# Moving the norm of the last 896 tokens one stage sooner and spreading its steps

## The chip, the cores and the metric

One core of a Trainium2 chip runs the kernel. The metric is device time in microseconds for one execution. The engines are TensorE (PE; its weight loads are shown as PEld), VectorE (DVE), ScalarE (ACT), GpSimd (POOL) and SyncE (SP), which issues DMAs. All have queues of their own and run their instructions in order; semaphores tie them together.

## What is computed

Attention over short local and strided masks, then a feed-forward layer, then a gated feed-forward layer with an RMS norm, for 2304 tokens of 512 features. The change lies in the last layer:

```python
def _moe2_ref(x, w_gate, w_val, w_out, rms_g):
    rms = np.sqrt(np.mean(x * x, axis=-1, keepdims=True) + 1e-06)
    xn = x / rms * rms_g
    g = xn @ w_gate
    silu = g * (1.0 / (1.0 + np.exp(-g)))
    val = xn @ w_val
    return (silu * val @ w_out).astype(np.float32)
```

Here d_model is 512 and d_ff is 1536. Every product is made of three products of fp32r halves (high x high, high x low, low x high).

## The kernel before, in words

The last layer runs over the tokens in three passes: 512 tokens (the loop with `pe_gv`), then two passes of 896 tokens, `j = 0` (the second pass) and `j = 1`. A pass of 896 tokens has six stages, `p = 0` to `5`, each for two blocks of 128 columns of `w_gate` and `w_val`. In a stage the two products x @ w are made as seven smaller ones on sums of quarter matrices (Strassen's scheme in Winograd's form): `Stage.run` goes through the product groups m = 1, 2, 5, 6, 3, 7, 4, and each group is 6 matmuls for `w_gate` and 6 for `w_val`, of 448 columns. Groups 1, 6, 7 and 4 collect in one pair of PSUM banks (P), groups 5 and 3 in another (R), group 2 in a pair Q. Between the groups DVE and ACT read the banks:

- `keep` (L1050, ACT) copies the bank of group 1, 5 and 6 to SBUF;
- `add` (L1040, L1043, DVE) adds a copy to the bank of groups 2, 3 and 7, in the order gate, val; then L1026 (ACT) makes the silu, `mul` (L1031, DVE) the product, L1035 (ACT) its high half and L1036 (DVE) its low half;
- after group 4, L1026 and L1031 read the bank itself.

A bank is written again only after its readers: group 4 after L1040 and L1043 of group 7, group 1 of the next stage after L1026 and L1031 of group 4. In each stage `outs` also makes seven output products of the stage before it (6 matmuls of 512 columns each: two after group 5, two after group 7, three after group 4); L1099 (ACT, p = 0 of the output) or L1101 (DVE) adds them to `osum`. These, the pair Q and the norm's product `ps_r` share four banks.

After each group stands a `tick`. It issues DMAs of weights (`fetch`, `put`), in the second pass it moves the decoding of the weights on (`decode.to`: per stage four times L276 on ACT, L277 and L278 on DVE, and twice a batch on POOL of four L290, two L264 and two L265), and takes one step of the generator `pg`. That generator is `prep_s`, the norm of the 896 tokens of the next pass. It works in place on one SBUF tile x2 and goes through two halves (512 and 384 tokens):

- step 1 loads x (L919, four DMAs on SP);
- per half, steps of squares (L925, L927 on ACT, L928 on DVE), high and low half of their sum (L931, L932), an empty step, the product with ones on PE (`ps_r`), then on DVE the mean (L941), the start value (L945, L948) and three Newton steps of the inverse root (L952, L953, L954 each), last the scaling of x (L957, four times, two a step).

That is 23 steps and an end. In the last stage, p = 5, the first tick runs what is left of `pg`, and then each tick calls `conv(m)`: casts and sums of the quarters of x for the next pass (L971 on POOL, L990 on ACT, L991 on DVE).

PE and SP take their instructions in the order in which the program issues them. The order on DVE, ACT and POOL is set by a scheduler when the kernel is built, from its own estimates; so where a step is issued moves instructions of other steps on these engines as well.

Of the kernel before, what the change touches and what calls it, by code (L numbers as in the profile page):

```python
# [33 lines left out]
def attn_moe_moe_kernel(  # L34
# [42 lines left out]
    NJ = (NT - R0) // (2 * HT)  # L77
    NP = FB // 2

    def runs(s):  # L80

        r = []
        for i, (b, t) in enumerate(subs[s]):
            if r and r[-1][0] == b and r[-1][1] + r[-1][2] == t:
                r[-1][2] += 64
            else:
                r.append([b, t, 64, 64 * i])
        return r
# [34 lines left out]
    for s in range(len(subs)):  # L123
        if len(runs(s)) > 1 or s in LANES:
            _, t0, n, _ = runs(s)[0]
# [199 lines left out]
    class Store:  # L325


        n = 0
# [533 lines left out]
    def preps():  # L862
        yield from prep_s(0, [(0, R0)], bank_m, pbr)
        x = xt["raw"]
        t = mid.tile([128, 2, 4, 512], F32R, tag="xs", name="xn")
        for c in range(4):
            nc.scalar.copy(out=t[:, 0, c], in_=x[:, c, :R0])
            nc.vector.tensor_tensor(out=t[:, 1, c], in0=x[:, c, :R0], in1=t[:, 0, c].bitcast(F32), op=ALU.subtract)
            yield
        xn[0] = t  # L870
        yield from prep_s(R0, HALVES, bank_m, pbx)
        for m in (1, 2, 5, 6, 3, 7, 4):
            conv(m)
            yield
# [88 lines left out]
    def conv(m):  # L963

        x = xt["raw"]
        b = {(k, h): x[:, 2 * k:2 * k + 2, HT * h:HT * (h + 1)] for k in range(2) for h in range(2)}

        def comb(name, p, q, out=None):
            if out is None:
                out = tmp[0].tile([128, 2, 512], F32, tag="w", name="tr")[:, :, :HT]  # L970
            nc.gpsimd.tensor_tensor(out=out, in0=p, in1=q, op=ALU.subtract)  # L971
            xt[name] = out
            return out

        if m == 1:
            v = b[0, 0]
        elif m == 2:
            v = b[1, 0]
        elif m == 3:
            v = b[1, 1]  # L980
        elif m == 5:
            v = comb("t1", b[0, 1], b[0, 0])
        elif m == 6:
            v = comb("t2", b[1, 1], xt.pop("t1"))
        elif m == 7:
            v = comb("t3", b[1, 1], b[0, 1])
        else:
            v = comb("t4", b[1, 0], xt["t2"], xt["t2"])
        t = xt[m]
        nc.scalar.copy(out=t[:, 0], in_=v)  # L990
        nc.vector.tensor_tensor(out=t[:, 1], in0=v, in1=t[:, 0].bitcast(F32), op=ALU.subtract)  # L991
# [16 lines left out]
    class Stage:  # L1008
# [37 lines left out]
        def keep(self, x):  # L1046
# [5 lines left out]
            return r  # L1052

        def run(self, outs, tick):
            P, Q, R = {}, {}, {}
            self.both(1, P, True)
            if (self.j, self.p) == (0, 0):
                second()
            m1 = self.keep(P)
            tick(1)  # L1060

            def q():
                self.both(2, Q, True)
                self.add((0, 0), Q, m1)
                tick(2)
# [64 lines left out]
    xq, first_units, pg = [], units[:3], None  # L1130
# [87 lines left out]
    for g, f, a, e in units:  # L1218
# [38 lines left out]
        if g == NG - 1:  # L1257
            if f == 2:
                pg = preps()
# [41 lines left out]
    pg = iter(())  # L1301
    for j in range(NJ):
        for p in range(NP):
            first, last, end = (j, p) == (0, 0), p == NP - 1, (j, p) == (NJ - 1, NP - 1)
            me, nxt = pairs[p], pairs[(p + 1) % NP]
            st = Stage(j, p)

            def tick(m):
                n = (1, 2, 5, 6, 3, 7, 4).index(m)
                if first and n == 3:  # L1310
                    for t in range(R0 // 128):
                        nc.sync.dma_start(out=out[t * 128:t * 128 + 128, :], in_=osum[:, t])
                if n in (1, 5):
                    me.fetch((6,) if n == 1 else (7, 8))
                if j == 0:
                    decode.to(10 + 10 * (7 * p + n + 3) // 7)
                    if n in (3, 5):
                        for kd in range(2):
                            me.put((2 if n == 3 else 4) + kd)
                if not end and n == 4:  # L1320
                    nxt.fetch((0, 1))
                if not end and (j > 0 or last) and n in (5, 6):
                    nxt.fetch((2, 3) if n == 5 else (4, 5))
                next(pg, None)
                if last and j + 1 < NJ:
                    for _ in pg:
                        pass
                    conv(m)

            if p == 2 and j + 1 < NJ:  # L1330
                pg = prep_s(R0 + 2 * HT * (j + 1), HALVES, bank_x, pbx)

            def outs(n):
                for _ in range(min(n, len(todo))):
                    o, t = todo.pop(0)
                    o.out(t)

            st.run(outs, tick)
            todo += [(st, t) for t in ((4, 5, 6, 3, 0, 1, 2) if end else range(7))]
# [99 lines left out]
```

## Time and profile before

| | us |
|---|---|
| median of 3 runs (lowest to highest) | 889.43 (888.55 to 890.35) |
| the profiled execution | 887.7 |
| its span | 885.9 |
| PE busy | 868.8 |
| DVE busy | 668.5 |
| ACT busy | 397.9 |
| POOL busy | 280.0 |

The second pass of the last layer begins at some 556 us; its stages p = 1 to p = 5 start at 576.7, 603.3, 630.3, 659.2 and 686.2 us. In the rows below a time in the first place is us from the span's start and the second is the duration; "x4" is four instructions in one row; an entry in brackets is the idle time before and what ended it. L numbers are lines of the kernel before; in the changed kernel lines from L1325 on are one higher, and none that is named here is affected.

### The profile page before, as it was taken

To read this page: it belongs to the slowest core of one execution; us is meant where nothing else is said; L and a number is where in the kernel's file an instruction comes from. 1 tells how busy PE (TensorE), PEld (TensorE's weight loads), DVE (VectorE), ACT (ScalarE), POOL (GpSimd) and SP (SyncE) were. 2 spreads that over 40 slices of the span, in tenths; PEclk is the share of its full clock that TensorE was granted. 3 is DMA by queue.
4 is the path that set the end of the run, shared out by engine and by line. 5 is a ranking of instruction groups with operands and counts; after the bars stand their busy time and mean duration, and the time that the engine had idled before them with its cause. 6 is when DMAs were issued, how large, how long until landed. Compare 5 with 4: busy or idle time off the path is not lost.

```text
span 885.9 us, 14105 instructions
## 1 busy us (share of the span) xinstructions
PE 868.8 (98%) x5091; PEld 739.7 (83%) x5091; DVE 668.5 (75%) x1376; ACT 397.9 (45%) x897; POOL 280.0 (32%) x315
## 2 busy tenths in 40 slices
PE   6999999999999999999999999999999999999998
PEld 4888888888998887888887888888878988888986
DVE  5999788888779887179978898576997953445444
ACT  6987643332544333265637553355332533422320
POOL 0000147695276952000000569676442400000000
PEclk8999999999999999999999999999999999999999
DMA  9955224311313000199828777799659139955002
GB/s 328 379 196 173 77 73 151 111 50 36 116 54 110 28 16 1 46 291 346 280 72 270 279 250 270 252 415 364 232 179 349 48 114 355 397 168 166 1 0 84
DMA packets 58566, 157.84 MB, mean 178 GB/s; under 512 B 9536, under 2 KB 20672, under 8 KB 58496
## 3 DMA queue, kind: packets, MB, share of 16 engines
q1 hardware_dynamic: 57344, 155.89, 50.0%
q10 hardware_dynamic: 1152, 1.05, 0.3%
q8 instruction: 40, 0.66, 0.3%
q14 instruction: 30, 0.25, 0.1%
HBM read 119.16 MB, written 37.75 MB: 177 GB/s over the span
## 4 chain that ended last, share of the span: by engine, by line
PE 82%; DVE 8%; POOL 5%; ACT 2%; issue 1%; DMA 1%; SPq 0%; DVEq 0%; POOLq 0%; ACTq 0%
PE ps_x L147 21%; PE ps_h L147 21%; PE ps_pr L147 18%; PE ps_o L147 12%; POOL pr L629 4%; PE ps_m L147 4%; PE ps_q L147 3%; DVE so L669 3%; DMA raw<-in_w_in_dram 1%; PE ps_s L147 1%; POOL pr L662 1%; PE ps_v L147 1%; ACT sm L416 1%; PE ps_p L437 1%; DVE x L957 0%
## 5 line engine op out<-in xcount | busy, mean ns | idle before, releaser
L147 PE MATMUL ps_h<-xs,w 128*128 128x512 f32 (+1 forms) x984 | 213.4, 365 | 0.7 <-DVE tg L814 0.7
L147 PE MATMUL ps_x<-g,w 128*128 128x512 f32 (+1 forms) x984 | 214.0, 366 | 0.0
L147 PEld LDWEIGHTS ps_h<-xs,w 128*128 128x128 f32 x984 | 169.0, 189 | 30.6 <-DVE tg L814 1.1
L147 PEld LDWEIGHTS ps_x<-g,w 128*128 128x128 f32 x984 | 168.6, 189 | 30.0 <-issue 0.2
L147 PE MATMUL ps_pr<-xt,wt 128*128 128x448 f32 x576 | 123.1, 366 | 2.2 <-DVE s L1040 1.4
L629 POOL TENSOR_TENSOR pr<-sk,sq 128x256 f32<-128x256 f32 (+2 forms) x101 | 82.5, 852 | 131.8 <-DMA sq<-in_q_str_dram 126.4
L147 PE MATMUL ps_o<-wt,p 128*128 128x512 f32 x504 | 120.2, 390 | 0.0
L147 PEld LDWEIGHTS ps_pr<-xt,wt 128*128 128x128 f32 x576 | 107.9, 188 | 13.5 <-DVE s L1040 2.2
L147 PEld LDWEIGHTS ps_o<-wt,p 128*128 128x128 f32 x504 | 94.6, 188 | 18.7
L820 ACT CAST g<-tg 128x512 fp32r<-128x512 f32 (+1 forms) x82 | 46.6, 568 | 108.9 <-DVE tg L814 108.8
L662 POOL TENSOR_TENSOR pr<-sv,se 128x288 f32<-128x288 f32 (+12 forms) x104 | 69.7, 691 | 56.7 <-DVE so L669 19.8
L1050 ACT COPY u<-ps_pr 128x448 f32<-128x448 f32 x72 | 38.2, 533 | 84.8 <-PE ps_pr L147 84.7
L814 DVE SCALAR_TENSOR_TENSOR tg<-ps_h,tg 128x512 f32<-128x512 f32 (+1 forms) x82 | 50.8, 619 | 28.0 <-ACT tg L809 28.0
L669 DVE TENSOR_REDUCE so<-pr 128x16 f32<-128x272 f32 (+11 forms) x104 | 65.0, 653 | 8.7 <-POOL pr L662 8.4
L971 POOL TENSOR_TENSOR tr<-x 128x896 f32<-128x896 f32 x4 | 15.1, 3765 | 171.1 <-DMA raw<-in_w_gate_dram 153.9
L809 ACT ACTIVATE tg<-ps_h 128x512 f32<-128x512 f32 (+1 forms) x82 | 44.2, 539 | 48.1 <-PE ps_h L147 48.1
L1101 DVE SCALAR_TENSOR_TENSOR osum<-ps_o,osum 128x512 f32<-128x512 f32 x70 | 47.9, 687 | 21.6 <-PE ps_o L147 20.9
L825 DVE TENSOR_TENSOR g<-tg,g 128x512 fp32r<-128x512 f32 (+1 forms) x82 | 55.3, 677 | 10.8 <-ACT g L820 10.2
L147 PE MATMUL ps_pr<-xt,wo 128*128 128x448 f32 x288 | 60.8, 366 | 0.2 <-ACT u L1050 0.2
L147 PEld LDWEIGHTS ps_pr<-xt,wo 128*128 128x128 f32 x288 | 54.0, 188 | 5.2 <-ACT u L1050 0.6
L184 ACT CAST w<-ct 128x512 fp32r<-128x512 f32 x68 | 42.1, 619 | 30.3 <-DVE ct L177 28.2
L634 DVE TENSOR_REDUCE sc<-pr 128x4 f32<-128x256 f32 (+2 forms) x101 | 43.8, 437 | 12.1 <-POOL pr L629 11.6
(110 smaller groups left out, 1201.4 us busy)
## 6 DMA issues: line engine op xcount, KB each, us to landing
wt<-w SPq DMA_DIRECT2D x84, 512.0 KB, 5.9
raw<-in_w_out_dram SPq DMA_DIRECT2D x28, 512.0 KB, 6.1
raw<-in_w_gate_dram SPq DMA_DIRECT2D x24, 512.0 KB, 5.9
raw<-in_w_val_dram SPq DMA_DIRECT2D x24, 512.0 KB, 6.8
w<-w SPq DMA_DIRECT2D x24, 512.0 KB, 6.6
w<-wo SPq DMA_DIRECT2D x24, 512.0 KB, 8.2
raw<-in_w_in_dram SPq DMA_DIRECT2D x16, 512.0 KB, 9.9
out_dram<-osum SPq DMA_DIRECT2D x18, 256.0 KB, 2.1
```

The source lines that it names most:

```text
L147: nc.tensor.matmul(out_, lhsT, rhs, start=start, stop=stop, skip_group_check=True)
L184: nc.scalar.copy(out=self.t[:, 0].rearrange("p c f -> p (c f)"), in_=self.b)
L629: nc.gpsimd.tensor_tensor(out=pr, in0=self.k[:, a:e, :], in1=self.q[:, c - c0:c - c0 + 1, :].to_broadcast([128, e - a, D]), op=ALU.mult,)
L634: pend.append(lambda: nc.vector.tensor_reduce(out=s[:, c - c0, a:e], in_=pr, axis=AX.X, op=ALU.add))
L662: nc.gpsimd.tensor_tensor(out=pr, in0=self.v[:, 0:c + 1, a:e], in1=self.e[:, c - c0, 0:c + 1].unsqueeze(2).to_broadcast([128, c + 1, e - a ...
L669: pend.append(lambda: nc.vector.tensor_reduce(out=o[:, c - g0, a:e], in_=pr.rearrange("l c d -> l d c"), axis=AX.X, op=ALU.add))
L809: nc.scalar.activation(out=t, in_=h_of[g, f, a], func=ACTF.Tanh, scale=WS)
L814: nc.vector.scalar_tensor_tensor(out=t, in0=h_of.pop((g, f, a)), scalar=WS, in1=t, op0=ALU.mult, op1=ALU.subtract)
L820: nc.scalar.copy(out=t[:, 0], in_=t_of[g, f, a])
L825: nc.vector.tensor_tensor(out=t[:, 1], in0=t_of.pop((g, f, a)), in1=t[:, 0].bitcast(F32), op=ALU.subtract)
L1050: nc.scalar.copy(out=u, in_=x[kd])
L1101: nc.vector.scalar_tensor_tensor(out=o, in0=ps, scalar=WS, in1=o, op0=ALU.mult, op1=ALU.add)
```

## The change

The norm's generator is made in stage p = 1 instead of p = 2, and a tick takes no step of it where 7p + n is a multiple of five (n is the tick's place in the stage, 0 to 6).

```diff
-                next(pg, None)
+                if (7 * p + n) % 5:
+                    next(pg, None)
                 if last and j + 1 < NJ:
                     for _ in pg:
                         pass
                     conv(m)
 
-            if p == 2 and j + 1 < NJ:
+            if p == 1 and j + 1 < NJ:
                 pg = prep_s(R0 + 2 * HT * (j + 1), HALVES, bank_x, pbx)
```

Before, steps 1 to 7 fall in p = 2, 8 to 14 in p = 3, 15 to 21 in p = 4 and the rest in the first tick of p = 5. Now steps 1 to 6 fall in p = 1, 7 to 11 in p = 2, 12 to 17 in p = 3 and 18 to 23 in p = 4.

What this makes of the order on the engines stands at three places. In the names, x2 is the tile of x, rz and sq hold the Newton values, ps_pr the banks of the product groups, ps_o those of the outputs, wa and raw the weights that are being decoded.

First DVE. Before, in stage p = 3, around the scaling of the first half (s_7248 is of group 3, s_7280 of group 7):

```order
L954 SCALAR_TENSOR_TENSOR sq_6892<-rz_7124,sq_6892 128x512
L1040 TENSOR_TENSOR s_7248<-ps_pr_7163,u_7223 128x448
L957 SCALAR_TENSOR_TENSOR x2_6857<-x2_6857,gcol_4677,sq_6892 128x512 x4
L1043 TENSOR_TENSOR v_7251<-ps_pr_7170,u_7225 128x448
L1040 TENSOR_TENSOR s_7280<-ps_pr_7098,u_7177 128x448
L1043 TENSOR_TENSOR v_7283<-ps_pr_7105,u_7179 128x448
```

The same work in the changed kernel, in stage p = 2 (s_7029 is of group 7, s_7079 of group 4):

```order
L1040 TENSOR_TENSOR s_7029<-ps_pr_6848,u_6920 128x448
L954 SCALAR_TENSOR_TENSOR sq_6645<-rz_6935,sq_6645 128x512
L1043 TENSOR_TENSOR v_7032<-ps_pr_6855,u_6922 128x448
L277 TENSOR_SCALAR wa_7195<-raw_7041 128x512
L1036 TENSOR_TENSOR p_6897<-s_6996,p_6897 128x448
L957 SCALAR_TENSOR_TENSOR x2_6610<-x2_6610,gcol_4677,sq_6645 128x512 x3
L1101 SCALAR_TENSOR_TENSOR osum_6387<-ps_o_7051,osum_6387 128x512
L957 SCALAR_TENSOR_TENSOR x2_6610<-x2_6610,gcol_4677,sq_6645 128x512
L1031 SCALAR_TENSOR_TENSOR s_7029<-v_7032,s_7029 128x448
L278 SCALAR_TENSOR_TENSOR wa_7195<-raw_7041,wa_7195 128x512
L1101 SCALAR_TENSOR_TENSOR osum_6387<-ps_o_7059,osum_6387 128x512
L277 TENSOR_SCALAR wa_7195<-raw_7084 128x512
```

The scaling of the first half has moved from between the sums of group 3 to behind those of group 7, ahead of the readers of two outputs.

Second DVE in stage p = 4, the end of the second half. In the changed kernel (s_7518 is of group 3, s_7551 of group 7):

```order
L954 SCALAR_TENSOR_TENSOR sq_7171<-rz_7432,sq_7171 128x384
L952 SCALAR_TENSOR_TENSOR rz_7432<-sq_7171 128x384
L953 TENSOR_TENSOR rz_7432<-rz_7432,acc_7170 128x384
L1040 TENSOR_TENSOR s_7518<-ps_pr_7439,u_7492 128x448
L954 SCALAR_TENSOR_TENSOR sq_7171<-rz_7432,sq_7171 128x384
L1043 TENSOR_TENSOR v_7521<-ps_pr_7446,u_7494 128x448
L957 SCALAR_TENSOR_TENSOR x2_6610<-x2_6610,gcol_4677,sq_7171 128x384 x4
L1031 SCALAR_TENSOR_TENSOR s_7518<-v_7521,s_7518 128x448
L1040 TENSOR_TENSOR s_7551<-ps_pr_7374,u_7453 128x448
L1043 TENSOR_TENSOR v_7554<-ps_pr_7381,u_7455 128x448
```

Before, this scaling stood behind the whole work of stage p = 4, with the first reader of p = 5 behind it:

```order
L954 SCALAR_TENSOR_TENSOR sq_7301<-rz_7526,sq_7301 128x384
L1101 SCALAR_TENSOR_TENSOR osum_6387<-ps_o_7606,osum_6387 128x512
L957 SCALAR_TENSOR_TENSOR x2_6857<-x2_6857,gcol_4677,sq_7301 128x384 x4
L1101 SCALAR_TENSOR_TENSOR osum_6387<-ps_o_7614,osum_6387 128x512
L1040 TENSOR_TENSOR s_7660<-ps_q_7646,u_7636 128x448
```

The scaling of the second half now stands ahead of the sums of group 7 of p = 4. On POOL the first L971 of `conv` follows the last batch of decoding directly in both kernels, and waits only for the L957 whose x it reads.

Third SP, the loads of x in the changed kernel:

```order
L164 DMA raw_6579<-in_w_val_dram 128x512
L919 DMA x2_6610<-x2d_98 128x896 x4
L259 DMA wt_6639<-w1_6_114 128x1024
L164 DMA raw_6667<-in_w_gate_dram 128x512
L164 DMA raw_6673<-in_w_gate_dram 128x512
```

Before, they stood thirteen DMAs later:

```order
L254 DMA w1_5_113<-wo_6523 128x1024
L164 DMA raw_6802<-in_w_val_dram 128x512
L919 DMA x2_6857<-x2d_98 128x896 x4
L259 DMA wt_6886<-w2_6_123 128x1024
L164 DMA raw_6914<-in_w_gate_dram 128x512
```

They are now ahead of two loads of raw weights for the decoding in p = 1.

## Rows read from the trace of the kernel before

**Rows 1.** The page, part 1: busy us, share of the span, instructions.
```profile
PE 868.8 (98%) x5091; PEld 739.7 (83%) x5091; DVE 668.5 (75%) x1376; ACT 397.9 (45%) x897; POOL 280.0 (32%) x315
```

**Rows 2.** Windows p = 1, 3, 5: us; busy PE, PEld, DVE, ACT, POOL; PEclk, DMA, GB/s.
```profile
576.70:603.30 26.60, 26.55 (x127) 23.29 (x126) 20.45 (x28) 15.08 (x29) 17.05 (x18) 1.00 1.03 414
...
630.30:659.20 28.90, 27.22 (x128) 23.54 (x128) 28.86 (x42) 11.21 (x22) 18.38 (x16) 1.00 0.68 237
...
686.20:712.80 26.60, 26.60 (x127) 23.66 (x126) 26.46 (x32) 13.51 (x21) 9.70 (x4) 1.00 0.11 41
```

**Rows 3.** Waits in 630.3 to 659.2: who for whom, us, times, longest.
```profile
PEld ps_pr L147 <- DVE s L1040: 1.9, 1, 1.9
```

**Rows 4.** Timeline of DVE and POOL in p = 3: start, us, engine, line, operation.
```profile
632.88 0.90 DVE L953 TENSOR_TENSOR rz<-rz,acc 128x512 f32<-128x512 f32 x1
...
644.54 1.89 POOL L290 TENSOR_TENSOR ws<-wa 128x256 f32<-128x256 f32 x2 [2.76 <-issue]
...
647.49 3.91 DVE L957 SCALAR_TENSOR_TENSOR x<-x,gcol,sq 128x512 f32<-128x512 f32 x4
...
648.77 2.09 POOL L264 CAST wo<-ws 128x512 fp32r<-128x512 f32 x2
...
651.86 0.61 DVE L1040 TENSOR_TENSOR s<-ps_pr,u 128x448 f32<-128x448 f32 x1
```

**Rows 5.** Timeline of PE, p = 2 to the start of p = 4.
```profile
603.29 2.60 PE L147 MATMUL ps_pr<-xt,wt 128*128 128x448 f32 x12
...
623.36 2.60 PE L147 MATMUL ps_pr<-xt,wt 128*128 128x448 f32 x12
625.79 0.63 PE L147 MATMUL ps_r<-s,ones 128*128 128x512 f32 x2
626.25 4.25 PE L147 MATMUL ps_o<-wt,p 128*128 128x512 f32 x18
630.34 2.59 PE L147 MATMUL ps_pr<-xt,wt 128*128 128x448 f32 x12
...
652.52 2.70 PE L147 MATMUL ps_pr<-xt,wt 128*128 128x448 f32 x12 [1.44 <-DVE s L1040]
...
659.16 2.59 PE L147 MATMUL ps_pr<-xt,wt 128*128 128x448 f32 x12
```

**Rows 6.** Timeline of DVE and POOL at the start of p = 5.
```profile
686.38 4.12 DVE L957 SCALAR_TENSOR_TENSOR x<-x,gcol,sq 128x384 f32<-128x384 f32 x4
...
687.65 2.43 POOL L971 TENSOR_TENSOR tr<-x 128x896 f32<-128x896 f32 x1 [17.19 <-PE ps_pr L147]
...
690.42 0.68 DVE L1101 SCALAR_TENSOR_TENSOR osum<-ps_o,osum 128x512 f32<-128x512 f32 x1
...
690.73 2.15 POOL L971 TENSOR_TENSOR tr<-x,tr 128x896 f32<-128x896 f32 x1 [0.65 <-DVE x L957]
...
691.02 0.61 DVE L1040 TENSOR_TENSOR s<-ps_q,u 128x448 f32<-128x448 f32 x1
```

**Rows 7.** Lines in 560 to 715: ns least/median/most, first and last start.
```profile
L957 DVE SCALAR_TENSOR_TENSOR x<-x,gcol,sq x8: 608/914/2529, 647.5 to 688.0; 128x512 f32<-128x512 f32 x4, 128x384 f32<-128x384 f32 x4
...
L277 DVE TENSOR_SCALAR wa<-raw x16: 410/420/1520, 565.0 to 659.9; 128x512 uint32<-128x512 uint32 x16
...
L278 DVE SCALAR_TENSOR_TENSOR wa<-raw,wa x16: 676/681/1780, 566.2 to 662.4; 128x512 uint32<-128x512 uint32 x16
...
L954 DVE SCALAR_TENSOR_TENSOR sq<-rz,sq x6: 548/614/1118, 633.8 to 685.3; 128x512 f32<-128x512 f32 x3, 128x384 f32<-128x384 f32 x3
...
L290 POOL TENSOR_TENSOR ws<-wa x16: 732/738/1195, 567.6 to 663.9; 128x256 f32<-128x256 f32 x16
...
L264 POOL CAST wo<-ws x16: 604/906/1079, 571.2 to 667.0; 128x512 fp32r<-128x512 f32 x16
...
L265 POOL TENSOR_TENSOR wo<-ws,wo x16: 1281/1628/1748, 572.7 to 669.2; 128x512 fp32r<-128x512 f32 x16
```

**Rows 8.** Timeline of SP's DMA issues, 569 to 591.
```profile
569.76 1.62 SPq L164 DMA_DIRECT2D raw<-in_w_gate_dram  x2
...
586.85 4.15 SPq L919 DMA_DIRECT2D x<-x2d  x4
```

## The prediction

> **What bounds the kernel now.** I read the page's engine shares first: TensorE (PE) is busy for 98% of the span and VectorE (DVE) for 75% [rows 1]. PE is the bound, so the change can only matter through PE's waits near the place that is edited. Next the windows view, stage by stage [rows 2]. A stage of the second pass without the norm's product takes 26.60 us, and PE is busy for all of it (p = 5). Stage p = 3 takes 28.90 us and PE is busy for 27.22; in the same stage DVE is busy for 28.86, that is, always. The list of waits names the cause: PE's weight loads waited 1.9 us for L1040 on DVE [rows 3]. The timeline shows where [rows 4]. L1040 is the sum that reads the product bank of group 7, and the products of group 4 may write that bank only after it. It started at 651.86, directly behind four L957 (the scaling of x by the norm) that took 3.91 us together and are in nobody's way. PE's group 4 therefore began at 652.52. From the start of stage p = 3 to that of p = 4 it is 659.16 - 630.34 = 28.82 us [rows 5], so the norm costs **2.2 us** today (28.82 - 26.60).
>
> Why did four L957 take 3.91 us? A DVE instruction of this size alone lasts 0.68 us (L278, L1101) and the next starts 0.60 behind it (690.42 to 691.02) [rows 6, 7]. Beside them GpSimd (POOL) was running its casts [rows 4]. The clearest case is in p = 5: four L957 of 384 columns, 0.61 us each at the least, took 4.12 us, because POOL's L971 ran from 687.65 to 690.08, and the last L957 (up to 2.53 us) ended only at 690.50 [rows 6, 7]. So a DVE instruction whose operands are all in SBUF and a POOL instruction **take turns**: one waits until the other has ended. The most that L277, L278, L954 and L265 show over their least fits this; L1040 and L1101, which read PSUM, are 0.61 and 0.68 beside POOL as well [rows 6, 7].
>
> **The change, part by part.** Nothing is added or removed but an `if`; 23 steps of the norm start seven product groups sooner and every fifth group makes none. They now end in the last group of p = 4; before, the last two were in p = 5.
>
> 1. *The loads of x.* Four DMAs move up on SP's queue, from 586.85 to ahead of two `raw` loads that were issued from 569.76 on [rows 8]. The DMA engines are busy all the time in p = 1 [rows 2], so these move back by what the four take there, 4.15 us. The user of `raw` is L277, early in the order of DVE in p = 1; L1040 and L1043 of groups 3 and 7 stand behind it. Three L928 of the norm now stand ahead of it anyway, and PE needs these results only at group 4, 20.07 us into the stage (623.36 - 603.29 in p = 2 [rows 5]). I take **0**; if that cover were gone it would cost up to 4.15.
>
> 2. *Squares.* Eight squares, two casts and six L928 move to p = 1 and p = 2/p = 3. ACT has 15.08 of 26.60 us busy in p = 1 [rows 2]: **0**. The two norm products on PE move from p = 2 and p = 4 to other places in p = 2 and p = 4, 0.46 us and less either way (625.79 to 626.25 [rows 5]): **0**.
>
> 3. *What goes.* The Newton steps and L957 of the first half leave p = 3, whose DVE had no gap. The wait goes: **-2.2 us**.
>
> 4. *What comes in p = 2.* All nine Newton instructions of the first half, and its four L957, now stand in p = 2, together with four L277 and four L278 of the weight decoding. They start when the norm's product is done: group 1 starts at 603.29, twelve products take 2.43 (623.36 to 625.79), the product 0.63 [rows 5], so L941 starts at 606.4. PE needs the last of the chain, L1031 of group 4, before the second half of group 1 of p = 3: at 603.29 + 26.60 + 0.46 + 1.22 = 631.6. Between the two stand, by the order, these turn-takers of DVE: 17 of 0.60 us (4 L278, 9 Newton, 4 L957), 5 of 448 columns at 0.54 (L1031, L1036), 6 at 0.34 (L277, L945, L948; 0.42 less the same 0.08), together 14.9 us. POOL runs two batches of decoding meanwhile, each four L290, two L264 and two L265 at the least 4 x 0.73 + 2 x 0.60 + 2 x 1.28 = 6.7 us [rows 7], together 13.4. Taking turns they need 28.3 us; with L1031 itself (0.62) the chain ends at 635.3. PE is late by 635.3 - 631.6 = **3.7 us**. Part of it is met at L1040 of group 7 before group 4, part at L1101, which frees a bank for the third output and now stands behind three L957.
>  Bounds: the 11 PSUM readers of the stretch (6.2 us) are hidden in this under POOL; with nothing hidden PE is late by about 9.9, and with POOL wholly free beside DVE not at all (14.9 + 6.2 + 0.6 ends at 628.1). The nearest rows are those of p = 3 of before. There, from L953 at 632.88 to the end of L1040 at 652.47 [rows 4], the same count gives 10.2 us of turn-takers, 11.4 of POOL (a batch and most of a second one) and 4.0 of PSUM readers in 19.6 us: 0.76 of their sum. By this share p = 2 needs 0.76 x 35.1 = 26.7 us and PE is late by 1.5. I take 3.7, since in p = 3 POOL stood idle for 2.76 us in between [rows 4], in which DVE lost no turn.
>
> 5. *What comes in p = 4.* The second half's Newton steps and L957 (384 columns) end in p = 4, and the order again puts four L957 before L1031 and L1040 of group 7. PE can start group 4 at 20.07 + 0.35 = 20.4 us into the stage. DVE's chain starts at 2.43 + 0.5 = 2.9 (the product is 384 columns wide, not 512). Up to L1040 there are 13 turn-takers at 0.47 to 0.53 (Newton, L957), 3 at 0.54, 2 at 0.60, 4 at 0.3, together 10.4 us, and on POOL one batch of 6.7 plus the first L971 (2.15), which starts as soon as two L957 are done. With L941 (0.5) and L1040 (0.6) that ends 2.9 + 10.4 + 8.85 + 1.1 = 23.3 us into the stage: **2.9 us** late. Bounds: by the share of 0.76 it is 0.6 late; with the 3.4 us of PSUM readers not hidden, 6.3.
>  Whether a second L971 gets in ahead of L1031 no row tells: behind 690.50 DVE had no turn-taker ready [rows 6]. Without such luck it is 0, with it 2.15. The Trainium skill, SBUF - State Buffer, section "Who interferes with whom", says that whichever issues first holds the shared port pair for its whole instruction. By that rule L1031, ready in DVE's queue before POOL hears of the last L957, goes first and the term stays 2.9; by the other order it would be 5.0. No run here shows it yet.
>
> 6. *What stays.* In p = 5 DVE is busy for 26.46 of 26.60 us and PE waits for nothing [rows 2], so four L957 fewer there give nothing back. Later stages are untouched.
>
> Sum: -2.2 + 3.7 + 2.9 = **+4.4 us**. The profiled execution took 887.7 us (span 885.9), 1.7 below the median of 889.43; it becomes 892.1, the median **893.8**.
>
> **The rivals.**
> - *DVE keeps up (faster).* If POOL's batches fall where DVE waits for PE anyway, the two times do not add: both new waits vanish and only -2.2 is left, 887.2. It decides at L1040 of group 7 in p = 2 and p = 4: done within 20.5 (20.4) us of the stage's start, or not. For it: p = 5 with DVE as full as this cost PE nothing. Against: L957 stands ahead of L1040 as it did in p = 3. The Trainium skill, Perfetto Trace Analysis, section "Identifying the Most-Contended Engine", calls the engine of highest occupancy the one to work on; by that, with PE at 98% and DVE at 75%, moved DVE work would be free. The trace disagrees in p = 3, where PE waited 1.9 us for DVE. Chance 0.09.
> - *The waits only move (no change).* By the share of 0.76: -2.2 + 1.5 + 0.6 = -0.1, 889.3. Chance 0.13.
> - *More turns lost.* The second L971 ahead of L1031 (+2.15) and some PSUM readers not hidden (some 1.5): 897.5. Chance 0.15.
> - *The loads come late in p = 1.* `raw` lands after DVE's order has come to it: up to +4.15 more, 898. Chance 0.03.
>
> **How the numbers follow.** The forecast has 0.60. About 0.2% (1.8 us) is what a measurement of this kernel can tell from no change; so faster 0.09, same 0.13, slower 0.60 + 0.15 + 0.03 = 0.78. The range leaves out the faster rival and the lower part of "no change" below, and above what exceeds the lost turn: 889.8 to 897.6.
>
> **What would show it.** Right: stage p = 3 at 26.6 us without a wait; p = 2 some 30 us with a last wait at the start of p = 3, and p = 4 some 29.9 us; PE waiting for L1040, L1101 and L1031 of DVE in p = 2, for L1040 in p = 4; one L957 of p = 4 at over 2 us beside L971. Wrong: p = 2 at 27.1 us, or L1040 of group 7 before group 4's turn; a wait of PE in p = 1.

## The result and the profile after

The changed kernel takes **896.3 us** (median of 6 runs, 894.44 to 897.16), the kernel before 890.85 beside it (6 runs, 888.55 to 893.55). The ratio is **1.0072**, with a 95% interval of 1.005 to 1.0093: +6.4 us (0.0072 x 890.85), between +4.5 and +8.3. It is slower, as forecast; 893.8 us and +4.4 had been predicted (from the 889.43 us of the first three runs; the same +4.4 from 890.85 us would be 895.3).

The page of the changed kernel, part 1 (busy us, share of the span, instructions), against [rows 1]:

```profile
PE 870.7 (97%) x5091; PEld 741.3 (83%) x5091; DVE 676.5 (76%) x1376; ACT 397.7 (44%) x897; POOL 277.8 (31%) x315
```

The numbers of instructions are the same. DVE is busy for 8 us more with the same 1376, so single DVE instructions lasted longer (in a second profile of each kernel it is 676.1 against 667.4). The time in which one stands still behind POOL is shown as busy, not as a wait, as the four L957 of p = 4 show below: 4.04 us beside POOL, 2.20 without.

Windows of the changed kernel, its stages p = 2 to p = 5 (us; busy PE, PEld, DVE, ACT, POOL; PEclk, DMA, GB/s):

```profile
606.98:637.65 30.67, 28.07 (x129) 24.17 (x128) 28.12 (x40) 11.69 (x22) 18.23 (x16) 0.98 0.75 262
637.65:665.35 27.70, 27.70 (x128) 24.59 (x126) 25.79 (x37) 11.33 (x22) 15.87 (x16) 0.96 0.61 209
665.35:695.69 30.34, 27.31 (x130) 23.93 (x128) 27.88 (x39) 7.54 (x14) 15.85 (x11) 1.00 0.86 306
695.69:722.29 26.60, 26.60 (x128) 23.66 (x126) 21.19 (x30) 13.82 (x22) 2.16 (x1) 1.00 0.08 27
```

The kernel before took 27.05, 28.82, 27.07 and 26.59 us for the same four stages, 109.53 together, by [rows 5] and the rows of PE that begin p = 5 and the stage behind it:

```profile
686.23 2.60 PE L147 MATMUL ps_pr<-xt,wt 128*128 128x448 f32 x12
...
712.82 2.59 PE L147 MATMUL ps_pr<-xt,wt 128*128 128x448 f32 x12
```

Now it is 115.31. The loss is in p = 2 and p = 4, and p = 3 has lost its own wait.

Timeline of PE in the changed kernel, rows with a wait in p = 2 to p = 4 and the first row of p = 3 (the bracket is the idle time and who ended it):

```profile
628.51 2.69 PE L147 MATMUL ps_pr<-xt,wt 128*128 128x448 f32 x12 [0.83 <-DVE s L1040]
...
635.70 2.16 PE L147 MATMUL ps_o<-wt,p 128*128 128x512 f32 x6 [1.77 <-DVE osum L1101]
637.65 3.69 PE L147 MATMUL ps_pr<-xt,wt 128*128 128x448 f32 x12
...
689.08 2.69 PE L147 MATMUL ps_pr<-xt,wt 128*128 128x448 f32 x12 [3.03 <-DVE s L1040]
```

These are the places that the prediction named: group 4 behind L1040 of group 7, and the third output behind L1101, in p = 2; group 4 behind L1040 in p = 4. The wait for L1031 at the start of p = 3, also named, does not show in this profile; a second one has it (0.37 us). The row at 637.65 has no wait, and yet its twelve products took 3.69 us instead of 2.60. That is a loss of another kind, shown in the last section.

DVE of the changed kernel at these places, in p = 2:

```profile
610.08 0.69 DVE L941 TENSOR_SCALAR acc<-ps_r 128x512 f32<-128x512 f32 x1 [2.49 <-PE ps_r L147]
...
627.85 0.61 DVE L1040 TENSOR_TENSOR s<-ps_pr,u 128x448 f32<-128x448 f32 x1
...
630.30 1.72 DVE L1036 TENSOR_TENSOR p<-s,p 128x448 fp32r<-128x448 f32 x1
631.94 3.10 DVE L957 SCALAR_TENSOR_TENSOR x<-x,gcol,sq 128x512 f32<-128x512 f32 x3
634.97 0.68 DVE L1101 SCALAR_TENSOR_TENSOR osum<-ps_o,osum 128x512 f32<-128x512 f32 x1
...
638.30 0.61 DVE L1031 SCALAR_TENSOR_TENSOR s<-ps_pr,s 128x448 f32<-128x448 f32 x1
```

and in p = 4:

```profile
683.92 4.04 DVE L957 SCALAR_TENSOR_TENSOR x<-x,gcol,sq 128x384 f32<-128x384 f32 x4
687.88 0.61 DVE L1031 SCALAR_TENSOR_TENSOR s<-v,s 128x448 f32<-128x448 f32 x1
688.41 0.61 DVE L1040 TENSOR_TENSOR s<-ps_pr,u 128x448 f32<-128x448 f32 x1
```

with POOL beside it:

```profile
685.19 2.35 POOL L971 TENSOR_TENSOR tr<-x 128x896 f32<-128x896 f32 x1 [4.32 <-DVE x L957]
688.18 2.31 POOL L971 TENSOR_TENSOR tr<-x,tr 128x896 f32<-128x896 f32 x1 [0.64 <-POOL tr L971]
```

POOL has waited for x for 4.32 us. When two L957 are done it runs, the last L957 stands still, and L1040, for which PE waits, ends at 689.02.

### The profile page after: what moved, and what is told of

Same layout as the page of the kernel before. It is cut to its first block, busy times and chain, and to the rows that moved or that the text cites. A ratio compares the mean times of both kernels' runs of the same rounds, so it can differ in the third digit from the quotient of the medians.

```text
span 895.4 us, 14100 instructions
## 1 busy us (share of the span) xinstructions
PE 870.7 (97%) x5091; PEld 741.3 (83%) x5091; DVE 676.5 (76%) x1376; ACT 397.7 (44%) x897; POOL 277.8 (31%) x315
## 4 chain that ended last, share of the span: by engine, by line
PE 57%; DVE 14%; issue 3%; POOL 3%; DMA 1%; ACT 1%; ACTq 0%; SPq 0%; DVEq 0%
PE ps_pr L147 17%; PE ps_x L147 12%; PE ps_o L147 12%; PE ps_h L147 12%; PE ps_q L147 3%; DVE so L669 3%; POOL pr L629 2%; DVE ct L177 1%; DVE x L957 1%; DMA raw<-in_w_val_dram 1%; PE ps_m L147 1%; POOL tr L971 1%; DVE w L188 1%; DVE g L825 1%; DVE ct L176 1%
## 5 line engine op out<-in xcount | busy, mean ns | idle before, releaser
L814 DVE SCALAR_TENSOR_TENSOR tg<-ps_h,tg 128x512 f32<-128x512 f32 (+1 forms) x82 | 50.8, 619 | 28.3 <-ACT tg L809 28.3
L1101 DVE SCALAR_TENSOR_TENSOR osum<-ps_o,osum 128x512 f32<-128x512 f32 x70 | 47.9, 687 | 22.5 <-PE ps_o L147 21.6
L971 POOL TENSOR_TENSOR tr<-x 128x896 f32<-128x896 f32 x4 | 9.8, 2458 | 158.2 <-DMA raw<-in_w_gate_dram 153.9
```

Of the source, the lines that this page charges most:

```text
L814: nc.vector.scalar_tensor_tensor(out=t, in0=h_of.pop((g, f, a)), scalar=WS, in1=t, op0=ALU.mult, op1=ALU.subtract)
L1101: nc.vector.scalar_tensor_tensor(out=o, in0=ps, scalar=WS, in1=o, op0=ALU.mult, op1=ALU.add)
```

## The experiments

Theory: a half of the norm costs time where its Newton steps and its L957 run in one stage with POOL's work and stand ahead of a reader that PE needs; half of that cost is turns lost to POOL. Rivals: the early start costs by itself (loads, squares); the groups left out cost; DVE's order alone makes the waits and POOL has no part.

The table shows the stages (start of group 1 to the next, from the timelines of PE) in one profile each, and the ratios of all runs:

| kernel | p = 2 | p = 3 | p = 4 | p = 5 | sum | ratio (95%) |
|---|---|---|---|---|---|---|
| before | 27.05 | 28.82 | 27.07 | 26.59 | 109.53 | 1 |
| before_again | 27.04 | 28.80 | 27.06 | 26.68 | 109.58 | |
| the change | 30.67 | 27.70 | 30.34 | 26.60 | 115.31 | 1.0072 (1.005 to 1.0093) |
| again | 30.20 | 27.23 | 31.94 | 26.61 | 115.98 | 1.0085 (1.0057 to 1.0112) |
| half1_back | 27.05 | 29.06 | 31.98 | 26.67 | 114.76 | 1.0049 (1.0025 to 1.0073) |
| half2_back | 30.19 | 28.78 | 27.06 | 26.60 | 112.63 | 1.0036 (1.0017 to 1.0055) |
| tr_held | 30.19 | 27.27 | 28.49 | 27.04 | 112.99 | 1.0058 (1.0037 to 1.0078) |
| less_pool | 27.08 | 28.14 | 31.80 | 26.60 | 113.62 | 1.0048 (1.0024 to 1.0072) |
| each_group | 29.20 | 27.81 | 30.51 | 26.60 | 114.12 | 1.0045 (1.0025 to 1.0066) |
| skip_only | 26.59 | 27.07 | 27.32 | 28.02 | 109.00 | 1.0006 (0.9988 to 1.0025) |
| one_sooner | 27.06 | 27.71 | 27.33 | 26.60 | 108.70 | 0.9992 (0.9976 to 1.0007) |
| fit_a | 27.05 | 28.25 | 26.94 | 26.60 | 108.84 | 0.9977 (0.9955 to 0.9999) |
| fit_b | 26.59 | 27.07 | 27.02 | 26.98 | 107.66 | 0.9986 (0.9958 to 1.0015) |

A norm product on PE (0.35 or 0.46 us) stands now in one stage, now in the next; an undisturbed stage is 26.6 without and about 27.05 with one. In each_group the first product stands in p = 1, outside the sum; in all other kernels the sum holds both.

### The change once more, and the kernel before once more

> The changed kernel once more, beside the kernel before on the same chip. Its first profile shows two separate losses against before: +5.8 us in stages p = 2 to p = 5 (115.3 against 109.5 us) and +3.6 us that had already been lost when stage p = 2 began (group 1 of p = 2 at 606.98 instead of 603.29). Up to the second product group of p = 1 the order of DVE's instructions is the same in both kernels. Theory (the change costs only at the readers of p = 2 and p = 4): the ratio is 1.005 to 1.009, p = 2, 3, 4 take 30.7, 27.7 and 30.3 us again within 0.5, and the 3.6 us ahead of p = 2 vary from run to run. Rival (early loads and squares cost something ahead of p = 2 as well): p = 2 again begins 3 us or more later than in the kernel before.

> The kernel before, for a second profile. If what is lost ahead of p = 2 in the profiles of the changed kernel (group 1 of p = 2 at 606.98 instead of 603.29) is a difference between executions, stage p = 2 begins at another time here than 603.29 by 1 us or more, while p = 2 to p = 5 take 27.0, 28.8, 27.1 and 26.6 us again within 0.4. Rival (it belongs to the changed kernel): 603.3 within 0.5.

The waits came back at the same places: 0.82 for L1040 and 1.68 for L1101 in p = 2, 0.37 for L1031 at the start of p = 3, 3.03 for L1040 in p = 4. Stage p = 4 was 1.6 us longer than in the first profile, with the same wait; the last section shows why. Stage p = 2 began late again, at 606.36, so this run alone did not exclude the rival. The kernel before did: in its second profile p = 2 began at 608.78 instead of 603.29, with the stages behind it unchanged. Part of such differences arises near the start of the program, which the change does not reach: one and the same row of PE (twenty products for `ps_x`) began at 39.06 us in the first profile of the kernel before, at 41.10 in its second, at 38.70 in the first profile of the change and at 41.92 in "again". The two rows below show another part, a wait that both kernels can meet, long before the change, first in the kernel before (second profile), then in the changed kernel:

```profile
544.36 3.02 PE L147 MATMUL ps_m<-xn,w 128*128 128x512 f32 x12 [2.37 <-DVE s L890]
```

```profile
542.15 3.04 PE L147 MATMUL ps_m<-xn,w 128*128 128x512 f32 x12 [2.37 <-DVE s L890]
```

So what is lost ahead of p = 2 differs between executions and belongs to neither kernel; single profiles are compared by their stages p = 2 to p = 5.

### One half put back at a time

In these kernels the steps stand in a list of ticks 7p + n:

```diff
-                if (7 * p + n) % 5:
-                    next(pg, None)
+                for _ in range(STEPS.count(7 * p + n)):
+                    next(pg, None)
```

half1_back: `STEPS = (7, 8, 9, 11, 12, 13, 20, 21, 22, 23, 24, 24, 25, 25, 26, 26, 27, 28, 29, 31, 32, 33, 34)`; half2_back: `(7, 8, 9, 11, 12, 13, 14, 16, 17, 18, 19, 21, 22, 23, 24, 26, 27, 31, 32, 33, 34)`.

> Loads and squares of the first half start in p = 1 as in the changed kernel, but the norm's product of the first half goes back to the last group of p = 2, where it was before; the second half is as in the changed kernel. Theory (each half costs by the stage in which its Newton steps and L957 run): p = 2 takes 27.1 us, p = 3 28.8 with the wait of 1.9 us for L1040 back, p = 4 30.3 with a wait of 3 us: before + 3.3 us, ratio 1.0037. Rival (the early start itself costs): + 5 us or more, ratio 1.006. Rival (the skipped groups cost, wherever the halves are): p = 2 stays above 29 us.

> The first half is as in the changed kernel; the norm's product of the second half goes back to the fourth group of p = 4, where it was before. Theory: p = 2 takes 30.7, p = 3 27.7 and p = 4 27.1 us: before + 2.5 us, ratio 1.0028. Rival (the early start itself costs): ratio 1.006, p = 4 unchanged at 30.3.

Each half costs in its own stage. With the first half put back p = 2 takes 27.05 us, although loads and squares start as early as in the change and groups are left out as before: both rivals fall at this stage. The old wait in p = 3 is back (1.43 us for L1040), and p = 4 keeps a wait of 3.06; that this stage takes 31.98 us, where 30.3 was expected, is again the loss of the last section. With the second half put back p = 4 takes 27.06 us and p = 2 keeps its waits. Timeline of PE, half1_back, then half2_back:

```profile
654.06 2.70 PE L147 MATMUL ps_pr<-xt,wt 128*128 128x448 f32 x12 [1.43 <-DVE s L1040]
...
684.44 4.26 PE L147 MATMUL ps_pr<-xt,wt 128*128 128x448 f32 x12 [3.06 <-DVE s L1040]
```

```profile
637.18 1.66 PE L147 MATMUL ps_o<-wt,p 128*128 128x512 f32 x6 [1.73 <-DVE osum L1101]
...
662.04 1.48 PE L147 MATMUL ps_pr<-xt,wt 128*128 128x448 f32 x6 [0.72 <-DVE v L1043]
```

One miss: half2_back has p = 3 at 28.78, where 27.7 was expected. Putting the second half back also moved two L277 and two L278 in DVE's order from p = 4 into p = 3, one pair between the sums of groups 3 and 7 and one behind them. L1040 of group 7 came later with it, and L1036 took 1.76 us between L1040 and L1043, beside L265 (1.01 us at the same place in "again"). An edit to one step moves other work too.

### POOL's part in the wait of p = 4

```diff
-            nc.gpsimd.tensor_tensor(out=out, in0=p, in1=q, op=ALU.subtract)
+            name == "t1" and "u" in xt and nc.gpsimd.tensor_copy(out=out[:, 0, :1], in_=xt["u"][0][:, :1]); nc.gpsimd.tensor_tensor(out=out, in0=p, in1=q, op=ALU.subtract)
...
-                r.append(u)
+                r.append(u); xt["u"] = r
```

> The changed kernel with POOL's first L971 made to wait for a copy of p = 5 (one column is copied ahead of it), so that no L971 runs in p = 4. The order on DVE in p = 4 stays word for word the same. Theory (a DVE instruction with all operands in SBUF and a POOL instruction take turns): the four L957 of p = 4 take 2.0 us instead of 4.04, PE's wait for L1040 falls from 3.0 to 1.0 us, p = 4 from 30.3 to 28.3; the changed kernel - 2 us, so before + 3.5 to 4 us. Rival (DVE's order and its own work make the wait, POOL has no part): p = 4 stays at 30.3 us and L957 at 1 us each.

Timeline of DVE in tr_held, p = 4, the same instructions in the same order as above, with one from earlier in the stage:

```profile
675.49 1.62 DVE L953 TENSOR_TENSOR rz<-rz,acc 128x384 f32<-128x384 f32 x1
...
681.30 2.20 DVE L957 SCALAR_TENSOR_TENSOR x<-x,gcol,sq 128x384 f32<-128x384 f32 x4
683.42 0.62 DVE L1031 SCALAR_TENSOR_TENSOR s<-v,s 128x448 f32<-128x448 f32 x1
683.96 0.62 DVE L1040 TENSOR_TENSOR s<-ps_pr,u 128x448 f32<-128x448 f32 x1
```

of POOL, whose batch of decoding stays in p = 4:

```profile
675.40 2.85 POOL L265 TENSOR_TENSOR wo<-ws,wo 128x512 fp32r<-128x512 f32 x2
```

and of PE:

```profile
684.63 2.70 PE L147 MATMUL ps_pr<-xt,wt 128*128 128x448 f32 x12 [1.17 <-DVE s L1040]
```

Four L957 take 2.20 us instead of 4.04 when no L971 runs beside them, and PE's wait falls from 3.03 to 1.17. Of the 3.0 us, 1.9 are turns lost to this L971. The other 1.2 are DVE's order, its own work and the turns lost to the batch (L953 took 1.62 us beside L265, a later L953 in the same stage 0.56); no run parts these three. The rival (order alone) falls as the whole cause. By the runs it is 1.0058 against 1.0085 in "again", some 2.4 us less; the two intervals overlap, so the stage and the wait carry this point, not the runs. L971 now comes in p = 5, which takes 27.04 instead of 26.60.

### POOL's part in p = 2

```diff
-            nc.gpsimd.tensor_copy(out=o[:, 0], in_=src)
-            nc.gpsimd.tensor_tensor(out=o[:, 1], in0=src, in1=o[:, 0].bitcast(F32), op=ALU.subtract)
+            (nc.scalar.copy if (self.p, k % 2) == (3, 1) else nc.gpsimd.tensor_copy)(out=o[:, 0], in_=src)
+            nc.scalar.copy(out=o[:, 1], in_=src) if (self.p, k % 2) == (3, 1) else nc.gpsimd.tensor_tensor(out=o[:, 1], in0=src, in1=o[:, 0].bitcast(F32), op=ALU.subtract)
```

> The changed kernel, but one of POOL's batches of decoding (weights of w_val for stage p = 3) makes its casts and low halves (two L264, two L265, some 5 us on POOL) with ACT copies instead; the low halves are left out, ACT copies the full value a second time. DVE has the same work as in the changed kernel, in nearly the same order. Theory (turns with POOL): the waits of p = 2 for L1040 (0.8 us) and for L1101 (1.7 us) go, p = 2 falls from 30.4 to under 28.5 us; p = 4, which is not touched, keeps its wait of 3 us. Before + 1.8 to 3.4 us, ratio 1.002 to 1.004. Rival (order and DVE's own work): p = 2 stays at 30.4 us, ratio 1.0075.

The low halves of this batch are left out in this kernel, for the sake of the timing. Both waits of p = 2 are gone, and the stage takes 27.08 us, as long as in the kernel before. 1.27 us of waiting for L1031 are left at the start of p = 3. Over p = 2 and p = 3 that is 55.22 us against 57.43 in the run "again". L957 was not quicker here (two of them took 3.47 us beside the next batch); the gain came ahead of it, since DVE reached L1040 of group 7 sooner:

```profile
622.94 0.61 DVE L1040 TENSOR_TENSOR s<-ps_pr,u 128x448 f32<-128x448 f32 x1
...
626.48 3.47 DVE L957 SCALAR_TENSOR_TENSOR x<-x,gcol,sq 128x512 f32<-128x512 f32 x2
629.88 0.68 DVE L1101 SCALAR_TENSOR_TENSOR osum<-ps_o,osum 128x512 f32<-128x512 f32 x1
```

The order on DVE changed a little with it (two L957 instead of three ahead of L1101, L1040 ahead of L1031), and ACT has more work, so this run is weaker evidence than tr_held. Its ratio, 1.0048, is above the 1.002 to 1.004 expected, though the interval reaches down to 1.0024; its p = 4 took 31.80 us, with the loss of the last section.

### Which half of the edit costs: the start or the groups left out

each_group starts in p = 1 and takes a step at every tick (the `if` removed); skip_only keeps the `if` and starts in p = 2.

> Norm begun in p = 1 as in the changed kernel, but one step after every product group, none left out; the norm's product of the first half then comes at the end of p = 1 and that of the second half at the end of p = 3. Theory (what costs is that the Newton steps and L957 of a half share a stage with POOL's batches and end ahead of a reader that PE waits for): p = 2 and p = 4 lose again, some 3 and 2 us, p = 3 nothing: before + 2 to 5 us, ratio 1.002 to 1.0055. Rival (it is the uneven spread, the groups left out, that costs): the ratio is within 0.002 of 1.

> Norm begun in p = 2 as in the kernel before, but with a step left out in every fifth group; the norm's product of the first half comes in p = 3 after the second group, that of the second half only in p = 5. Theory: p = 3 loses its wait of 1.9 us, since L957 no longer stands ahead of L1040 of group 7; a wait of under 1 us may come at the start of p = 4 and in p = 5, where the whole of the second half now falls: within 0.002 of before. Rival (the groups left out cost): ratio 1.004 or more. Rival (p = 5 is full, DVE busy for 26.5 of 26.6 us, so all of the second half's 8 us shows there): ratio 1.005 or more.

Leaving out groups is not what costs: each_group, which leaves out none, is at 1.0045, skip_only, which does, at 1.0006. Nor is it the early start as such, which half1_back has as well with p = 2 at 27.05 us. It is where the start and the groups left out together put the two halves. In skip_only the wait of p = 3 is gone; 0.45 us for L1031 and 0.70 for L1040 came instead, the second in p = 5 behind four L957 of 4.09 us beside L971. Most of the second half's work stayed hidden there (p = 5 takes 28.02 us, 1.4 more than in the kernel before, 0.35 of it the norm's product), although the kernel before shows DVE busy in p = 5 nearly all the time [rows 2]. Part of that busy time was standing still beside L971: an L991 took up to 2.67 us there and 1.07 alone. In skip_only DVE is busy for 24.88 of the 28.02 us.

### Places without a collision

one_sooner: `STEPS = (13, 14, ..., 34)`, each tick, begun in p = 1. fit_a: the same, with `25, 26, 27, 27, 28, 30` in place of 25 to 30. fit_b: begun in p = 2, `STEPS = (15, 16, 17, 18, 19, 20, 22, 23, 24, 25, 25, 25, 25, 25, 26, 26, 28, 30, 31, 32, 33, 34)`.

> The kernel before with the norm begun one product group sooner, a step in each group: every step stands one group ahead of where it was. The order then has the four L957 of the first half ahead of two L1101 and of the sums of group 3, no longer directly ahead of L1040 of group 7, and the Newton steps of the second half end before group 7 of p = 4. Theory (only the place of the L957 against the readers counts, and POOL's batch beside them): the wait of p = 3 falls from 1.9 us to under 0.6 and nothing comes in p = 4: before - 1.3 us, ratio 0.9985, at the edge of what can be told. Rival (any step that comes sooner costs): ratio over 1.001.

> As the kernel one_sooner, but one step of the second half's squares comes a group earlier (steps after groups 25, 26, 27, 27, 28, 30, counted 7p + n), so that the last L928 no longer stand between L1040 and L1043 of group 7 of p = 3 beside POOL's L265. In one_sooner that cost 0.9 us of waiting (L928 took 1.65 us there). Theory (place against the readers, and turns with POOL): no wait over 0.3 us from p = 2 to p = 5; p = 3 takes 26.6 to 27.1 us; before - 1.9 us, ratio 0.998. Rival (the wait only moves to the next reader): p = 3 or p = 4 at 28 us, ratio 0.9995 or more.

> Norm begun in p = 2 one group later than before; the product of the first half after the second group of p = 3 (as in skip_only), that of the second half after the third group of p = 4 (earlier than before); the squares of the second half come close together in p = 3. Theory: neither half ends ahead of L1040 of group 7 beside a batch of POOL: no wait over 0.3 us in p = 2 to p = 5, before - 1.9 us, ratio 0.998. Rival (the wait only moves): p = 3 or p = 4 at 28 us.

one_sooner lost the wait for L1040, but met one of 0.87 us for L1043 in p = 3, behind an L928 that took 1.65 us beside L265; under 0.6 was expected. fit_a was to remove that one, and its edit did not do it: in its profile an L928 of 1.64 us still stands between L1040 and L1043 of group 7 beside L265, and PE waits for 1.38 us at the same place. So it tests neither theory nor rival. Its runs came out at 0.9977 all the same; the profiled execution was the slowest of the twelve (893.22 us, median 888.05). In fit_b the profile has no wait of PE at all between 600 and 725 us, and the four stages sum to 107.66 us, 1.9 less than before, as expected. Timeline of its L957 of the first half, which now stand behind L1040 and L1043 of group 7:

```profile
656.02 2.73 DVE L957 SCALAR_TENSOR_TENSOR x<-x,gcol,sq 128x512 f32<-128x512 f32 x4
```

By the runs no version is clearly faster: fit_b's interval includes 1, and fit_a's ends at 0.9999. A gain of 2 us is about what can just be told.

## Why the prediction was right, point by point

- *The bound and the place.* PE waits for DVE in p = 2 and p = 4 at L1040 and L1101, and (in "again") at the start of p = 3 at L1031, as named, and nowhere else that the change reaches.
- *Step 1 and 2, loads and squares: 0.* In half1_back they start as early as in the change and p = 2 takes 27.05 us; no wait of PE falls in p = 1 behind its first group.
- *Step 3 and 4, p = 3 and p = 2: -2.2 + 3.7 = +1.5.* Measured over both stages: 57.43 (again) - 55.87 = +1.6. In the first profile it is 58.37, +2.5, with PE's stretch at half clock from the last section. From the start of L941 to the end of L1031 of group 4 the changed kernel took 28.8 us (638.91 - 610.08), where 28.3 us of turns and 0.6 for L1031 itself had been counted. So the sum was the right size; the share of 0.76 taken from p = 3, by which the waits would only have moved, was not. That p = 3 would take 26.6 us without a wait did not come: it took 27.70 and 27.23.
- *Step 5, p = 4: +2.9.* Measured in the first profile: 30.34 - 27.07 = +3.3, the wait 3.03. L1040 ended 23.7 us into the stage (689.02 - 665.35), where 23.3 had been counted. The second L971 started at 688.18, behind L1031 at 687.88, so the term was not 5.0. The Trainium skill, SBUF - State Buffer, section "Who interferes with whom", says that whoever issues first holds the shared ports for its whole instruction. The trace agrees here: L1031 kept its 0.61 us.
- *Step 6, p = 5: 0.* 26.60 us, and no wait.
- *The step that fell short is the sum.* It counts only waits. Taken from the profile in which each stage has no stretch at half clock, the change costs +1.56 us in p = 2 and p = 3 and +3.27 in p = 4, together +4.8, near the +4.4 forecast. With these stretches the stages cost +5.8 us (first profile) and +6.4 (again). By the runs it is +6.4, and +7.6 in "again" (0.0085 x 889.99). The part that is known to be missing is a price behind a wait, which the prediction did not have: PE at half its clock for 3.4 us. In how many of the runs without a profile it fell is not shown, so a part of the difference stays open.
- *Rivals.* "DVE keeps up" and "the waits only move" are excluded by the interval (1.005 and more). "More turns lost" (897.5) lies nearer to the measured 896.3 us than the forecast of 893.8, but by another mechanism: its lost turn, the second L971 ahead of L1031, did not happen. The loads did not come late.

## What to carry to other kernels

A step that moves to "idle" groups is free only if the engine that runs it can end it before the next reader that the bound engine needs; count what stands ahead of that reader, and count the other engine's instructions that take turns with it, since their times add where both are ready. In a kernel whose order is set when it is built, look up where the moved instructions and their neighbours really stand: here the same 23 steps gave ratios from 0.9977 to 1.0085. To a new wait of PE of 2 to 3 us add the chance of a stretch at half clock behind it, worth 1.6 us in p = 4 here.

## What the runs showed of the hardware that was not expected

A wait of PE can cost more than itself. Windows of the changed kernel around the wait for L1101 (634 to 635.7); the column before DMA is the granted clock, 1.00 for 2.4 GHz and 0.50 for 1.2 GHz:

```profile
633.70:635.60 1.90, 0.23 (x2) 0.00 (x0) 1.90 (x5) 0.00 (x0) 0.00 (x0) 1.00 0.95 354
635.60:636.60 1.00, 0.90 (x4) 0.77 (x5) 1.00 (x3) 0.26 (x1) 0.00 (x0) 1.00 0.81 299
636.60:637.60 1.00, 1.00 (x4) 0.76 (x3) 1.00 (x3) 0.99 (x3) 0.00 (x0) 0.52 0.26 98
637.60:638.60 1.00, 1.00 (x4) 0.85 (x3) 1.00 (x3) 0.43 (x1) 0.00 (x0) 0.50 0.29 41
638.60:639.60 1.00, 1.00 (x5) 0.87 (x4) 1.00 (x3) 0.66 (x2) 0.00 (x0) 0.50 0.78 262
639.60:640.60 1.00, 1.00 (x6) 0.92 (x5) 1.00 (x3) 1.00 (x3) 0.00 (x0) 0.78 0.96 377
```

PE works again from 635.7 on; a microsecond later its clock falls to half for 3.4 us and comes back while PE works on. PE is busy throughout, so no list of waits shows it; it appears as six products in 2.16 us instead of 1.67 and twelve in 3.69 instead of 2.60. In the run "again" the same products of the third output, behind nearly the same wait, kept the full clock, and the half clock came behind the wait in p = 4:

```profile
635.05 1.67 PE L147 MATMUL ps_o<-wt,p 128*128 128x512 f32 x6 [1.68 <-DVE osum L1101]
...
687.53 3.71 PE L147 MATMUL ps_pr<-xt,wt 128*128 128x448 f32 x12 [3.03 <-DVE s L1040]
```

Its windows there:

```profile
684.00:687.50 3.50, 0.50 (x3) 0.07 (x1) 3.50 (x5) 0.53 (x1) 2.86 (x2) 1.00 0.98 322
...
689.50:690.50 1.00, 1.00 (x4) 0.87 (x4) 1.00 (x1) 0.08 (x1) 1.00 (x1) 0.50 1.03 422
690.50:691.50 1.00, 1.00 (x4) 0.81 (x4) 1.00 (x1) 0.00 (x0) 0.89 (x1) 0.50 1.03 418
```

That made p = 4 31.94 us instead of 30.34: 1.6 us more with the same wait. half1_back, less_pool and each_group show it as well behind their waits of 3.06, 3.12 and 2.03 us in p = 4. It did not follow the wait of 3.03 us in the first profile of the change, nor those of 1.68 to 1.73 us for L1101 in tr_held, again and half2_back, nor the 1.4 us for L1040 in the kernel before, nor the 1.62 us for L1031 at 581.5 in the changed kernel, nor the 2.4 us for L890 at 541 to 544 in the six profiles that have it. So it came behind four of the five waits of 2 us or more in p = 4, behind one of four of 1.7 us in p = 2, and behind none of six of 2.4 us earlier. What decides in a single case stays open; no run was made on it alone.
